# Chunk 0 of a gated attention written without moves, fewer filler products at the head, and joined products in later chunks

## The chip, the cores and the metric

The kernel runs on one core of one Trainium2 chip. The metric is device time in microseconds (us) of one execution; lower is better. Three timed executions of the kernel before gave 989.09, 989.59 and 989.59 us, median 989.59. Engines: PE is TensorE, DVE is VectorE, ACT is ScalarE, POOL is GpSimd, and SP issues the DMAs.

## What is computed

A gated linear attention (4 batches, 8 heads, 768 steps, 48 features a head) and then two feed-forward networks on its 3072 x 384 output:

```python
for t in range(S):
    state = alpha[:, :, t, :, None] * state + np.einsum('bhd,bhe->bhde', k[:, :, t], v[:, :, t])
    y[:, :, t] = np.einsum('bhd,bhde->bhe', q[:, :, t], state)
x = y.transpose(0, 2, 1, 3).reshape(B * S, H * D)
h = x @ w_in                                        # 384 -> 2048
x = np.where(h > 0, h, np.exp(np.minimum(h, 0)) - 1) @ w_out
g = x @ w_gate; val = x @ w_val                     # 384 -> 1536
return (g * sigmoid(g) * val) @ w_out2
```

All of it is float32. Large products are made of three float32r products, of high and low parts of both operands (`mm3`).

## The kernel before

The sequence is cut into 6 chunks of 128 steps, and a chunk of one batch is a **unit**: unit `u` is batch `u % 4` of chunk `u // 4`, 24 in all. Chunk 0 has no state yet, so units 0 to 3 do less than later ones. For each unit the kernel does, in the names used below:

- **load**: one DMA of 1 MB from `qkva` into a tile `in` of three buffers, with the decay F, the keys K, the queries Q and the values V. Unit 0's comes in two pieces, F (256 KB) and K, Q, V (768 KB). The tile is free for unit `u + 3` once all its readers are done.
- **decay** (methods `A`, `N`, `M`): DVE scans F (`scan`, 4 instructions), clamps it (`R<-in`), ACT makes a reciprocal, DVE and ACT refine it, and K and Q are scaled in place. From unit 4 on POOL does two of these products.
- **T**, transposes of K (`Dk`, 4 matmuls into PSUM, ACT copies them to `KT`); **S**, scores (`E`, 8 matmuls, DVE masks them into `A`); **O**, outer products of K and V (`Gs`, 8 matmuls, DVE adds them to the state `sc`); **V**, the values (`Hy`, first 4 matmuls with the state, not in chunk 0, then 8 with `A`). V's output is split into a high part (ACT) and a low part, both into the chunk's operand tile `x`. The low part is DVE's for units 4 to 23; for units 0 to 3 (`u < MINUS`) PE subtracts the high part with a product by minus the identity, and ACT copies what is left.

Of the 4 pairs of heads three lie in `x` as they come; the fourth goes to a side tile `x3`, and after each chunk `gaps` moves it with 6 DMAs into rows 48 to 63 and 112 to 127 of `x`. These rows are operands of every **h block** (`mm1`, 9 matmuls of 512 columns, then ACT and DVE make the activation `g`), and each h block is followed, two later, by an **acc block** (`mm2`, 9 matmuls that read `g`). Weights are prepared tile by tile: a DMA into one of two `raw` buffers, two passes of ACT, two of DVE (`merge`, `sign`), one of ACT and one of DVE (`wt<-raw,wt`); tile 2i is read by h blocks 2i and 2i + 1 of a chunk, tile 2i + 1 by their acc blocks. Chunks 0 and 1 go through the 2048 features in halves (`SEGMENTS`): 8 h and 8 acc blocks of chunk 0, the same of chunk 1, then the second halves. Then comes the second network, whose blocks are `gv` and `q`.

The order on each engine is not written by hand. `Plan.add` takes an operation's engine, an estimate of its time, what it reads and writes; `Plan.run` lists all of them by their longest way to the end and hands them out in that order, and `Pinned` keeps it. SP's DMAs are in one order too. While PE is planned to be idle before the first h block, `warm` puts **filler** in: products of a zero tile `wz` into `idle`, one for each 0.22 us of the planned gap. 30 more stand at the head (`at.warm(6.8)`), ahead of everything.

PSUM tags matter here: `aps` (one bank) takes T, O and V; `ape` (two banks) takes S; units 0 to 3 also use `acc0` to `acc2`.

In the trace nearly all instructions carry line L128 (the `Pinned` helper), so they are told apart by tiles: `aps<-ident,in` is T, `ape<-in` S, `aps<-in,KT` O, `aps<-in,sbd` and `aps<-A,in` V, `x<-x` the moves.

Of the kernel before, what the change touches and what calls it, by code (L numbers as in the profile page):

```python
# [8 lines left out]
F32 = mybir.dt.float32  # L9
F32R = mybir.dt.float32r  # L10
BF16 = mybir.dt.bfloat16
# [23 lines left out]
SEGMENTS += [(c, 0, NF1, (c + 1) % NCH) for c in range(2, NCH)]  # L35
MINUS = B
SOON, MARGIN = 40.0, 0.5
# [4 lines left out]
class Plan:  # L42
# [25 lines left out]
    def run(self, fill=None, until=0):  # L68
# [38 lines left out]
        for i in sorted(range(n), key=lambda i: (start[i], i)):  # L107
            if ops[i][0] == "PE" and fill and start[i] <= start[until]:
                fill(start[i] - last)
                last = start[i] + ops[i][1]  # L110
            ops[i][2]()
# [29 lines left out]
def kernel(  # L141
# [119 lines left out]
    class Attention:  # L261
        def __init__(self, es):
# [12 lines left out]
            self.bias = cp.tile([128, 2], F32, name="bias")  # L275
            self.neg = cp.tile([128, 128], F32R, name="neg")
            self.x3 = cp.tile([128, 2, TB], F32R, name="x3")
            self.u = {}
# [18 lines left out]

        def init(self):
            vec.memset(self.zero, 0.0)
# [13 lines left out]
            nc.gpsimd.tensor_copy(self.mask, t)  # L313
            for t in self.sbd:
                nc.gpsimd.memset(t, 0.0)

        def warm(self, us):

            if self.idle is None:
                self.z = self.cp.tile([128, 128], BF16, name="wz")  # L320
                vec.memset(self.z, 0.0)
# [96 lines left out]
        def Dk(self, u):  # L418
# [15 lines left out]

            plan.add("PE", 0.45, flip, r=[K], w=[key], soon=SOON, lag=MARGIN)
            plan.add("ACT", 0.48, keep, r=[key], w=["KT"])

        def E(self, u):
# [33 lines left out]

            plan.add("PE", 1.25, scores, r=[K, Q], w=keys, soon=SOON, lag=MARGIN)
            plan.add("DVE", 1.24 if len(keys) > 1 else 1.1, causal, r=keys, w=["A"])

        def Gs(self, u):
# [3 lines left out]
            c, b = divmod(u, B)  # L480
            key, bank = self.bank(u)
            sc = self.sc[b]

# [12 lines left out]
            def state():  # L496
# [6 lines left out]
                vec.tensor_tensor(out=sc[0:PR], in0=kv, in1=pc, op=ALU.mult)  # L503

            plan.add("PE", 0.75, outer, r=["KT", V], w=[key], soon=SOON, lag=MARGIN)
            plan.add("DVE", 0.65 if c else 0.3, state, r=[key, F], w=[("sc", b)])

        def Hy(self, u):
            d, (F, K, Q, V) = self.u[u], self.keys(u)
            c, b = divmod(u, B)  # L510
# [37 lines left out]
            def low():  # L548
# [7 lines left out]
            if u >= MINUS:  # L556
                plan.add("DVE", 0.74, low, r=[key], w=[xk, gk])
                return

            def minus():  # L560
                y, x3, x = parts()
                for i, h in ((slice(0, KD), x[0]), (slice(KD, NP), x3[0])):
                    ten.matmul(
                        out=d["oy"][0:PR, i.start * C:i.stop * C], lhsT=self.neg[0:PR, 0:PR],
                        rhs=h, start=False, stop=True, skip_group_check=True)

            def rest():
                y, x3, x = parts()
                act.activation(out=x3[1], in_=y[:, KD], func=AF.Copy)
                act.activation(out=x[1], in_=y[:, 0:KD], func=AF.Copy)  # L570

            plan.add("PE", 0.45, minus, r=[xk, gk], w=[key], soon=SOON)
            plan.add("ACT", 0.68, rest, r=[key], w=[xk, gk])

# [28 lines left out]
        def step(self, u):  # L603
# [5 lines left out]
            if nxt:  # L609
                self.N(u + 1)  # L610
            self.Gs(u)
# [8 lines left out]
            if nxt:  # L620
                self.Dk(u + 1)
# [3 lines left out]
    def new_x(c):  # L625
        xt[c] = P.xp.tile([128, 2, KD, TB], F32R, tag="x", name="x")
# [193 lines left out]
    w1, w2 = {}, {}  # L820
    at.warm(6.8)
    at.init()
# [241 lines left out]
```

## Time and profile before

| what | us |
|---|---|
| median of three timed runs | 989.59 |
| the profiled execution | 990.69 |
| its span (first to last instruction) | 988.9 |
| PE busy | 973.4 |
| DVE busy | 541.0 |
| ACT busy | 512.7 |
| POOL busy | 69.3 |

The sums below are made against the profiled execution, 990.69 us, of which 1.8 us lie outside the span. It is 1.1 us above the median; a difference found in it is taken from the median as it is. A busy PE is not PE at its peak, and filler counts as busy.

### The profile page before, as it was taken

What the parts mean: (1) busy time and instruction counts of PE and PEld (TensorE: products, weight loads), DVE (VectorE), ACT (ScalarE), POOL (GpSimd) and SP (SyncE); (2) the same over time, 40 slices, a digit from 0 to 9 for tenths busy, and PEclk for the clock granted to TensorE, in tenths of its full rate; (3) what the DMA queues carried; (4) which work ended last, traced back from release to release, by engine and by line L of the source; (5) the groups of instructions that cost most, each with busy time, mean ns of one, the idle gap of its engine ahead of it and who ended that gap; (6) DMA issues with size and microseconds to landing.
All of it is one profiled execution on the core that took longest, in us unless ns stands there. A gap on an engine that the chain in (4) does not pass through costs nothing.

```text
span 988.9 us, 13352 instructions
## 1 busy us (share of the span) xinstructions
PE 973.4 (98%) x5354; PEld 811.2 (82%) x5354; DVE 541.0 (55%) x840; ACT 512.7 (52%) x910; POOL 69.3 (7%) x51
## 2 busy tenths in 40 slices
PE   9899999999999999999999999999999999999997
PEld 4577788878887888888888888888888888888886
DVE  4999888667646653533677763334333334333332
ACT  3889999666776765555898542212212212212111
POOL 0122011123211310100000000000000000000000
PEclk9999999999999999999999999999999999999999
DMA  4646434333302301100434311001001001000001
GB/s 192 222 158 209 162 114 159 108 102 118 101 1 85 129 6 43 36 14 1 160 128 183 127 52 65 1 1 64 1 1 57 8 1 45 9 1 32 1 1 36
DMA packets 20662, 72.51 MB, mean 73 GB/s; under 512 B 2672, under 2 KB 5744, under 8 KB 17648
## 3 DMA queue, kind: packets, MB, share of 16 engines
q1 hardware_dynamic: 20592, 71.58, 21.2%
q8 instruction: 44, 0.72, 0.3%
q14 instruction: 26, 0.21, 0.1%
HBM read 58.20 MB, written 11.01 MB: 70 GB/s over the span
## 4 chain that ended last, share of the span: by engine, by line
PE 91%; ACT 3%; DVE 3%; DMA 2%; issue 0%; SPq 0%; ACTq 0%; DVEq 0%
PE gv L128 30%; PE acc L128 19%; PE h L128 18%; PE q L128 15%; PE aps L128 4%; PE idle L128 2%; PE ape L128 2%; DMA in<-qkva 1%; DVE in L128 1%; ACT raw L128 1%; DVE raw L128 1%; DMA raw<-w 1%; ACT e L128 1%; ACT R L128 1%; ACT x L128 0%
## 5 line engine op out<-in xcount | busy, mean ns | idle before, releaser
L128 PE MATMUL gv<-x,wt 128*128 128x512 f32 x1296 | 308.1, 391 | 0.0
L128 PEld LDWEIGHTS gv<-x,wt 128*128 128x128 f32 x1296 | 242.2, 188 | 48.0
L128 PE MATMUL h<-x,wt 128*128 128x512 f32 x864 | 215.6, 394 | 1.4 <-DMA x<-x 1.4
L128 DVE TENSOR_TENSOR s<-gv,s 128x512 f32<-128x512 f32 x144 | 99.6, 691 | 210.7 <-ACT s L128 167.3
L128 PE MATMUL acc<-g,wt 128*128 128x512 f32 x864 | 214.5, 393 | 0.2 <-DVE g L128 0.2
L128 PEld LDWEIGHTS h<-x,wt 128*128 128x128 f32 x864 | 159.7, 188 | 37.0 <-ACT r L128 1.7
L128 PEld LDWEIGHTS acc<-g,wt 128*128 128x128 f32 x864 | 160.4, 188 | 35.0 <-DVE g L128 0.6
L128 PE MATMUL q<-wt,u 128*128 128x384 f32 x864 | 163.0, 337 | 0.0
L128 PEld LDWEIGHTS q<-wt,u 128*128 128x128 f32 x864 | 153.6, 188 | 5.6
L128 ACT ACTIVATE s<-gv 128x512 f32<-128x512 f32 x72 | 43.1, 598 | 176.6 <-PE gv L128 176.6
L128 DVE SCALAR_TENSOR_TENSOR e<-e,r 128x512 f32<-128x512 f32 x96 | 68.6, 715 | 98.0 <-ACT r L128 97.9
L128 ACT ACTIVATE u<-s 128x512 fp32r<-128x512 f32 x72 | 45.4, 631 | 123.6 <-DVE s L128 123.2
L128 ACT ACTIVATE e<-h 128x512 f32<-128x512 f32 x96 | 57.1, 595 | 67.8 <-PE h L128 67.4
L128 DVE TENSOR_TENSOR g<-e,g 128x512 fp32r<-128x512 f32 x96 | 67.3, 701 | 29.8 <-ACT g L128 29.5
L128 ACT ACTIVATE g<-e 128x512 fp32r<-128x512 f32 x96 | 60.3, 628 | 28.9 <-DVE e L128 28.5
L128 DVE SCALAR_TENSOR_TENSOR raw<-raw 128x768 int32<-128x768 int32 x68 | 67.9, 1000 | 12.0 <-ACT raw L128 10.9
L128 DVE TENSOR_TENSOR u<-s,u 128x512 fp32r<-128x512 f32 x72 | 49.8, 692 | 40.6 <-ACT u L128 40.5
L128 ACT ACTIVATE e<-e 128x512 f32<-128x512 f32 x96 | 60.7, 632 | 2.9
L128 ACT ACTIVATE raw<-raw 128x768 f32<-128x768 f32 x68 | 58.9, 905 | 3.1 <-DMA raw<-w 2.9
L128 ACT ACTIVATE r<-h 128x512 f32<-128x512 f32 x96 | 55.9, 582 | 0.0
L128 POOL TENSOR_TENSOR in<-in 112x512 f32<-112x512 f32 x20 | 30.1, 1504 | 249.9 <-DVE in L128 130.7
L128 POOL TENSOR_TENSOR in<-in,R 112x512 f32<-112x512 f32 x20 | 37.0, 1849 | 79.5 <-ACT R L128 79.5
(78 smaller groups left out, 614.7 us busy)
## 6 DMA issues: line engine op xcount, KB each, us to landing
raw<-w SPq DMA_DIRECT2D x34, 768.0 KB, 4.2
in<-qkva SPq DMA_DIRECT2D x23, 1024.0 KB, 5.4
x2r<-x2d SPq DMA_DIRECT2D x18, 256.0 KB, 3.4
out<-y SPq DMA_DIRECT2D x24, 192.0 KB, 2.0
x2d<-o SPq DMA_DIRECT2D x12, 256.0 KB, 2.3
x<-x SPq DMA_DIRECT2D x36, 64.0 KB, 4.3
half<-o SPq DMA_DIRECT2D x6, 256.0 KB, 4.0
part<-half SPq DMA_DIRECT2D x6, 256.0 KB, 6.1
```

The source lines that it names most:

```text
L128: ins = getattr(self.engine, name)(*a, **k)
```

## The change

**Chunk 0 without moves.** A new method `first` takes the place of `Hy` for units 0 to 3. POOL copies parts of V (`apart`, 128 x 96) into a zeroed tile `vz`, and 4 more matmuls a unit add the fourth pair of heads straight into the rows where the moves put them. So one ACT copy, one subtraction on PE and one ACT copy are left where there were two of each, and `gaps` is not called for chunk 0. (That V's first 8 matmuls become 6, of 64 rows, and 6 more read `vz`, 12 in all.)

**Joined operations.** For units 4 to 19 T is part of the operation S, right behind it, and O part of V, right behind it, and O's output goes to `ape` instead of `aps`.

**Filler.** The 30 at the head are gone; `warm` now gets the start of the gap, and puts one for each 0.25 us into the first gap and one for each 0.36 us into later ones.

```diff
-MINUS = B
 ...
-                fill(start[i] - last)
+                fill(start[i] - last, last)
 ...
+            self.vz = cp.tile([128, 2, KD, 64], F32, name="vz")
 ...
+            nc.gpsimd.memset(self.vz, 0.0)
 ...
-        def warm(self, us):
+        def warm(self, us, start):
...
-            for _ in range(int((us - 0.2) / 0.22)):
+            for _ in range(int((us - 0.2) / (0.25 if start else 0.36))):
 ...
             # Dk
-            plan.add("PE", 0.45, flip, r=[K], w=[key], soon=SOON, lag=MARGIN)
-            plan.add("ACT", 0.48, keep, r=[key], w=["KT"])
+            if u < B:
+                plan.add("PE", 0.45, flip, r=[K], w=[key], soon=SOON, lag=MARGIN)
+                plan.add("ACT", 0.48, keep, r=[key], w=["KT"])
+            return key, flip, keep
...
             # E
-            plan.add("PE", 1.25, scores, r=[K, Q], w=keys, soon=SOON, lag=MARGIN)
+                def both():
+                    scores()
+                    flip()
+                plan.add("PE", 1.65, both, r=[K, Q], w=[*keys, key], soon=SOON, lag=MARGIN)
+                plan.add("ACT", 0.48, keep, r=[key], w=["KT"])
...
             # Gs
+            if c:
+                key, bank = ("ape",), lambda: self.pe.tile(
+                    [128, 2, 512], F32, tag="ape", name="ape")[:, 0]
...
+        def first(self, u):
...
+            def apart():
+                pool.tensor_copy(
+                    self.vz[:, :, :, D:64],
+                    d["v"][:, 2 * KD:H, 0:D].rearrange("p j (i e) -> p j i e", i=KD))
...
+                for p in range(KD):
+                    for j in range(2):
+                        ten.matmul(
+                            out=o[64 * j:64 * j + 64, p * C:(p + 1) * C], lhsT=self.vz[:, j, p],
+                            rhs=d["A"][:, j, KD], start=False, stop=p == KD - 1)
...
+            plan.add("POOL", 0.4, apart, r=[V], w=["vz"], port=True)
+            plan.add("PE", 1.5, values, r=["A", V, "vz"], w=[key], soon=SOON, lag=MARGIN)
+            plan.add("ACT", 0.45, high, r=[key], w=[xk])
+            plan.add("PE", 0.25, minus, r=[xk], w=[key], soon=SOON)
+            plan.add("ACT", 0.45, rest, r=[key], w=[xk])
...
         def Hy(self, u):
+            if u < B:
+                self.first(u)
+                return
...
-            plan.add("PE", 2.0 if c else 1.4, values, r=["A", V, Q, ("sbd", u % 2)], w=[key],
-                     soon=SOON, lag=MARGIN)
+            renew = self.Gs(u)
+            if renew:
+                okey, outer, state = renew
+                def both():
+                    values()
+                    outer()
+                plan.add("PE", 2.35, both, r=["A", V, Q, "KT", ("sbd", u % 2)], w=[key, okey],
+                         soon=SOON, lag=MARGIN)
+                plan.add("DVE", 0.65, state, r=[okey, F], w=[("sc", b)])
...
-            if b == B - 1:
+            if b == B - 1 and c:
                 self.gaps(c)
...
-    at.warm(6.8)
     at.init()
```

The plan makes a new order of this. On DVE, from the first scan to the mask of unit 0's scores (`A<-acc`); `scan` prints as `in<-in,zero`. Before:

```order
L128 SCALAR_TENSOR_TENSOR in<-in,zero 112x128 x4
L128 TENSOR_SCALAR R<-in 112x512
L128 TENSOR_TENSOR in<-in 112x512
L128 SCALAR_TENSOR_TENSOR N<-in,R 112x512
L128 TENSOR_TENSOR in<-in,R 112x512
L128 SCALAR_TENSOR_TENSOR in<-N,in 112x512
L128 SCALAR_TENSOR_TENSOR in<-in,zero 112x128 x4
L128 TENSOR_SCALAR R<-in 112x512
L128 TENSOR_TENSOR in<-in 112x512
L128 TENSOR_TENSOR A<-acc_245,mask 128x512
```

and now:

```order
L127 SCALAR_TENSOR_TENSOR in<-in,zero 112x128 x4
L127 TENSOR_SCALAR R<-in 112x512
L127 SCALAR_TENSOR_TENSOR in<-in,zero 112x128 x4
L127 SCALAR_TENSOR_TENSOR N<-in,R 112x512
L127 TENSOR_TENSOR in<-in 112x512
L127 TENSOR_TENSOR in<-in,R 112x512
L127 SCALAR_TENSOR_TENSOR in<-N,in 112x512
L127 TENSOR_TENSOR in<-in 112x512
L127 TENSOR_SCALAR R<-in 112x512
L127 SCALAR_TENSOR_TENSOR in<-in,zero 112x128 x4
L127 TENSOR_TENSOR in<-in 112x512
L127 TENSOR_TENSOR A<-acc_217,mask 128x512
```

Unit 1's scan moves ahead of unit 0's scaling, and unit 2's scan and one more scaling now stand before the mask.

On SP, the first loads of the program (x512 is unit 0's F, x1536 under `in` its K, Q and V, x2048 a whole unit, `raw` a weight tile). Before:

```order
L128 DMA in<-qkva 128x512
L128 DMA in<-qkva 128x1536
L128 DMA in<-qkva 128x2048 x2
L128 DMA raw<-w 128x1536 x2
L128 DMA in<-qkva 128x2048 x2
```

and now:

```order
L127 DMA in<-qkva 128x512
L127 DMA in<-qkva 128x2048
L127 DMA in<-qkva 128x1536
L127 DMA in<-qkva 128x2048
L127 DMA raw<-w 128x1536 x2
```

Unit 1's megabyte has gone ahead of unit 0's K, Q and V.

On PE, unit 9 (one of the units 4 to 19) between h and acc blocks; eight matmuls of O alternate in the two shapes shown. Before:

```order
L128 MATMUL aps<-ident,in 128x112 x4
L128 MATMUL h<-x,wt 128x512 x9
L128 MATMUL aps<-in,KT 64x48
...
L128 MATMUL acc_1556<-g,wt 128x512 x3
...
L128 MATMUL aps<-in,sbd_116 112x128 x4
L128 MATMUL aps<-A,in 64x128
...
L128 MATMUL h<-x,wt 128x512 x9
```

and now:

```order
L127 MATMUL ape<-in 128x128 x8
L127 MATMUL aps<-ident,in 128x112 x4
L127 MATMUL acc_1472<-g,wt 128x512 x3
...
L127 MATMUL aps<-in,sbd_116 112x128 x4
L127 MATMUL aps<-A,in 64x128
...
L127 MATMUL ape<-in,KT 64x48
...
L127 MATMUL h<-x,wt 128x512 x9
```

T, O and V were three interruptions of the blocks, and S a fourth elsewhere; now there are two.

## Rows read from the trace of the kernel before

**Rows 1.** The page: granted clock by slice, and the chain by engine.

```profile
PEclk9999999999999999999999999999999999999999
...
PE 91%; ACT 3%; DVE 3%; DMA 2%; issue 0%; SPq 0%; ACTq 0%; DVEq 0%
```

**Rows 2.** Timeline, PE: start, length, engine, line, tiles, shapes, count [idle before, releaser].

```profile
1.07 18.50 PE L128 MATMUL idle<-wz 128*128 128x512 bf16 x72 [1.07 <-DVE zero L128]
...
54.01 4.37 PE L128 MATMUL h<-x,wt 128*128 128x512 f32 x18
```

**Rows 3.** Timeline, DVE, from the first scan to the mask of unit 0.

```profile
4.77 1.37 DVE L128 TENSOR_TENSOR_SCAN in<-in,zero 112x128 f32<-112x128 f32 x4 [2.02 <-DMA in<-qkva]
...
7.77 0.69 DVE L128 TENSOR_TENSOR in<-in 112x512 f32<-112x512 f32 x1 [1.17 <-DMA in<-qkva]
8.38 0.69 DVE L128 SCALAR_TENSOR_TENSOR N<-in,R 112x512 f32<-112x512 f32 x1
...
20.76 1.29 DVE L128 TENSOR_TENSOR A<-acc,mask 128x512 int32<-128x512 int32 x2 [7.80 <-PE acc L128]
```

**Rows 4.** Busy time by stretch: length, then PE, PEld, DVE, ACT, POOL; clock, DMA share, GB/s.

```profile
9.00:10.00 1.00, 1.00 (x6) 0.48 (x5) 0.81 (x3) 0.87 (x2) 0.00 (x0) 1.00 0.97 410
...
60.00:80.00 20.00, 19.75 (x157) 15.67 (x154) 19.82 (x33) 19.81 (x38) 4.43 (x3) 1.00 0.49 184
80.00:100.00 20.00, 18.98 (x139) 15.26 (x137) 19.93 (x31) 18.58 (x35) 5.21 (x3) 1.00 0.64 199
100.00:150.00 50.00, 49.67 (x269) 40.82 (x270) 42.62 (x59) 46.52 (x80) 4.64 (x3) 1.00 0.40 136
```

**Rows 5.** Timeline, DVE: the second and the seventh low part of `g`.

```profile
71.32 0.66 DVE L128 TENSOR_TENSOR g<-e,g 128x512 fp32r<-128x512 f32 x1
...
100.94 0.68 DVE L128 TENSOR_TENSOR g<-e,g 128x512 fp32r<-128x512 f32 x1
```

**Rows 6.** Timeline, PE: second acc block; ninth h block, seventh and eighth acc blocks.

```profile
71.92 2.34 PE L128 MATMUL acc<-g,wt 128*128 128x512 f32 x9
...
100.33 2.35 PE L128 MATMUL h<-x,wt 128*128 128x512 f32 x9 [1.35 <-DMA x<-x]
102.52 2.20 PE L128 MATMUL acc<-g,wt 128*128 128x512 f32 x9
104.56 2.20 PE L128 MATMUL h<-x,wt 128*128 128x512 f32 x9
```

**Rows 7.** Timeline, PE, around unit 8's O, V and unit 9's S.

```profile
132.83 2.20 PE L128 MATMUL acc<-g,wt 128*128 128x512 f32 x9
134.96 0.67 PE L128 MATMUL aps<-in,KT 128*64 128x48 f32 x16
135.56 2.33 PE L128 MATMUL h<-x,wt 128*128 128x512 f32 x9
137.73 1.04 PE L128 MATMUL aps<-in,sbd 112*112 112x128 f32 x8
139.71 1.16 PE L128 MATMUL ape<-in 48*128 48x128 f32 x16
```

**Rows 8.** Timeline, PE's weight loads under the filler at the head.

```profile
1.90 0.15 PEld L128 LDWEIGHTS <-wz 128*128 128x128 bf16 x1 [0.28 <-issue]
...
6.59 12.48 PEld L128 LDWEIGHTS <-wz 128*128 128x128 bf16 x58 [0.28 <-issue]
```

**Rows 9.** POOL and DVE at 45 us, and POOL's copy of 128 x 128 at the head.

```profile
2.73 0.29 POOL L313 CAST mask<-mt 128x128 int32<-128x128 f32 x1
...
45.17 1.31 POOL L128 TENSOR_TENSOR in<-in,R 112x512 f32<-112x512 f32 x1 [2.10 <-ACT R L128]
...
45.27 1.76 DVE L128 SCALAR_TENSOR_TENSOR N<-in,R 112x512 f32<-112x512 f32 x1
```

**Rows 10.** Timeline, DVE and PE at the change from chunk 2 to chunk 3.

```profile
218.03 1.37 DVE L128 TENSOR_TENSOR_SCAN in<-in,zero 112x128 f32<-112x128 f32 x4 [4.23 <-DMA in<-qkva]
...
220.30 1.13 PE L128 MATMUL aps<-in,sbd 112*112 112x128 f32 x8 [0.88 <-DVE T L128]
```

More of the change, by code (lines that the diff above doesn't have):

```diff
@@ L298, in init @@
         def init(self):
+            self.z = self.cp.tile([128, 128], BF16, name="wz")
+            vec.memset(self.z, 0.0)
             vec.memset(self.zero, 0.0)
@@ L315, in init @@
                 nc.gpsimd.memset(t, 0.0)
-        def warm(self, us):
+        def warm(self, us, start):
             if self.idle is None:
-                self.z = self.cp.tile([128, 128], BF16, name="wz")
-                vec.memset(self.z, 0.0)
                 self.idle = ph.tile([128, TB], F32, tag="h", name="idle")
-            for _ in range(int((us - 0.2) / 0.22)):
+            for _ in range(int((us - 0.2) / (0.25 if start else 0.36))):
                 ten.matmul(
@@ L471, in causal @@
                     )
-            plan.add("PE", 1.25, scores, r=[K, Q], w=keys, soon=SOON, lag=MARGIN)
+            turned = self.Dk(u) if u >= B else None
+            if turned:
+                key, flip, keep = turned
+                def both():
[3 more added lines that the diff above has]
+                plan.add("ACT", 0.48, keep, r=[key], w=["KT"])
+            else:
+                plan.add("PE", 1.25, scores, r=[K, Q], w=keys, soon=SOON, lag=MARGIN)
             plan.add("DVE", 1.24 if len(keys) > 1 else 1.1, causal, r=keys, w=["A"])
@@ L503, in state, with values, high, minus @@
                 vec.tensor_tensor(out=sc[0:PR], in0=kv, in1=pc, op=ALU.mult)
+            if c:
+                return key, outer, state
             plan.add("PE", 0.75, outer, r=["KT", V], w=[key], soon=SOON, lag=MARGIN)
-            plan.add("DVE", 0.65 if c else 0.3, state, r=[key, F], w=[("sc", b)])
+            plan.add("DVE", 0.3, state, r=[key, F], w=[("sc", b)])
+        def first(self, u):
+            d, (F, K, Q, V) = self.u[u], self.keys(u)
+            key, bank = self.bank(u)
+            ts = slice(u * C, (u + 1) * C)
+            xk = ("x", 0, u)
+            def apart():
+                pool.tensor_copy(
+                    self.vz[:, :, :, D:64],
+                    d["v"][:, 2 * KD:H, 0:D].rearrange("p j (i e) -> p j i e", i=KD))
+            def values():
+                d["oy"] = o = bank()
+                for p in range(KD):
+                    for j in range(2):
+                        ten.matmul(
+                            out=o[64 * j:64 * j + 64, p * C:(p + 1) * C], lhsT=d["v"][:, 2 * p + j, :],
+                            rhs=d["A"][:, j, p], start=p == 0, stop=False)
+                for p in range(KD):
+                    for j in range(2):
+                        ten.matmul(
+                            out=o[64 * j:64 * j + 64, p * C:(p + 1) * C], lhsT=self.vz[:, j, p],
+                            rhs=d["A"][:, j, KD], start=False, stop=p == KD - 1)
+            def high():
+                if 0 not in xt:
+                    new_x(0)
+                act.activation(
+                    out=xt[0][:, 0, :, ts], in_=d["oy"][:, 0:KD * C].rearrange("p (a c) -> p a c", a=KD),
+                    func=AF.Copy)
+            def minus():
+                ten.matmul(
+                    out=d["oy"][:, 0:KD * C], lhsT=self.neg, rhs=xt[0][:, 0, :, ts],
+                    start=False, stop=True, skip_group_check=True)
+            def rest():
+                act.activation(
+                    out=xt[0][:, 1, :, ts], in_=d["oy"][:, 0:KD * C].rearrange("p (a c) -> p a c", a=KD),
+                    func=AF.Copy)
+            plan.add("POOL", 0.4, apart, r=[V], w=["vz"], port=True)
[3 more added lines that the diff above has]
+            plan.add("ACT", 0.45, rest, r=[key], w=[xk])
@@ L551, in low @@
                 vec.tensor_tensor(out=x[1], in0=y[:, 0:KD], in1=f32(x[0]), op=ALU.subtract)
-            plan.add("PE", 2.0 if c else 1.4, values, r=["A", V, Q, ("sbd", u % 2)], w=[key],
-                     soon=SOON, lag=MARGIN)
-            plan.add("ACT", 0.68, high, r=[key], w=[xk, gk])
[L556 to L573, printed above, removed]
+            renew = self.Gs(u)
[7 more added lines that the diff above has]
+                plan.add("DVE", 0.65, state, r=[okey, F], w=[("sc", b)])
+            else:
+                plan.add("PE", 2.0, values, r=["A", V, Q, ("sbd", u % 2)], w=[key],
+                         soon=SOON, lag=MARGIN)
+            plan.add("ACT", 0.68, high, r=[key], w=[xk, gk])
+            plan.add("DVE", 0.74, low, r=[key], w=[xk, gk])
         def check(self):
@@ L610, in step @@
                 self.N(u + 1)
-            self.Gs(u)
+            if u < B:
+                self.Gs(u)
             if nxt:
@@ L619, in step @@
                 self.load(u + INS)
-            if nxt:
+            if nxt and u + 1 < B:
                 self.Dk(u + 1)
```

## The prediction

> **What bounds the kernel now.** I read the chain of waits first: 91% of it is PE at a granted clock of 0.9 or more in every slice [rows 1]. So the end is PE's, and a change is worth what it takes from PE's stream or starts it earlier. The timeline of PE shows where the stream is not work: 72 filler products run from 1.07 to 19.57, and the first h block starts only at 54.01 [rows 2]. What feeds PE meanwhile is read on DVE. It does its first scan at 4.77 and is through with what it has at about 13, and then the mask of unit 0 finds it idle for 7.80 us, waiting for scores that stand in PE's queue behind the filler [rows 3]. So the filler costs, because it is longer than the time that it should fill. The table by stretch then tells who holds the pace afterwards: from 60 to 100 us DVE is busy for 39.75 of 40 us and ACT for 38.4, while from 100 to 150 DVE is busy for 42.6 of 50 [rows 4]. DVE, with ACT beside it, paces everything up to about 100 us; behind that PE alone does. Two rows show the hand-over: the seventh `g` is ready at 101.62 [rows 5], and the acc block that reads it starts at 102.52, 0.9 us later [rows 6], with no further wait for DVE behind it but one [rows 10].
>
> So a gain at the head is worth what it moves DVE, not what it moves PE, and I follow it to the seventh acc block at 102.52.
>
> **The head: DVE's lead.** The new head has 29 filler products in place of 72. In the trace the first are 0.43 us apart until 6.59, and then 58 weight loads take 12.48 us, 0.215 each [rows 8]. So 29 are over near 10.1 (13 slow ones to 6.6, 16 fast ones in 3.4), before there is anything to multiply, and the loads decide.
>
> The order of loads is new, and it is not in unit 0's favour. In the trace F and the 768 KB behind it, 1.05 MB, are on the chip when the scaling starts at 7.77 [rows 3], and transfers flow at 410 GB/s [rows 4]. If they land in the order of issue, F and unit 1 (1.31 MB) are there at 8.4, unit 0's K, Q, V (2.10 MB) at 10.3, unit 2 (3.15 MB) at 12.9. DVE's new order then runs: scan of unit 1 8.4 to 9.8; N, two scalings and the refinement at 0.61 each (the distance of two rows in [rows 3]) to 12.2, with K finished; scaling and clamp of unit 1 to 13.2; scan of unit 2 to 14.6; one scaling; mask at 15.2. PE does T and S from 12.2, in 1.7 us (S 1.16 [rows 7], T's four matmuls no more than the 0.6 of O's eight), so the scores are there at 14.0 and the mask doesn't wait. In the trace it starts at 20.76. That is 5.5 us earlier, with one scan (1.37) and one scaling (0.6) more done: **DVE leads by 7.5 us**.
>
> From there to the seventh `g` the two orders hold the same DVE operations but for these, counted row by row: up to the second `g` one more pair of `x` subtractions (0.76), up to the seventh two fewer weight passes (1.9). DVE is dense in the trace there, so its lead stays: the second `g`, 71.98 before [rows 5], comes at 71.98 - 7.5 + 0.76 = 65.2; the seventh, 101.62, at 101.62 - 7.5 - 1.9 = 92.2. ACT doesn't object: it has eight copies fewer to do by then (the fourth pair of chunk 0).
>
> PE's own way between these two: ten blocks stand between the second and the seventh acc block, at 2.04 (102.52 to 104.56, [rows 6]); two joint V and O at 2.7 (V 1.98, O 0.60, and 0.13 on the next block, [rows 7]) and one S and T at 1.7. That is 27.5, and 65.2 + 27.5 = 92.7, later than DVE's 92.2. So the seventh acc block starts at 92.7 and not at 102.52: **-9.8 us**.
>
> This holds also the end of two waits. The six moves of chunk 0 no longer stand between V of unit 3 and the first h block; by DVE's order that block starts near 42 instead of 54.01, 12 us earlier, but acc blocks can't follow faster than `g` comes, so the surplus is spent in waits of PE. It is hidden by DVE's pace; were DVE not the bound, it would be worth 2.5 more. And the ninth h block's wait of 1.35 us for chunk 1's moves [rows 6] goes, since V of unit 7 now stands five blocks ahead of it and not three: 10.2 us of cover for what took 7.8 (V's end at 92.5 to 100.33).
>
> **The joined products: -1.8 us.** Each piece of attention between blocks costs more than itself. The acc block ahead of O takes 2.13 (132.83 to 134.96) and the h block behind it 2.17, against 2.04: 0.22 for one interruption [rows 7]. Counted in the orders from the ninth h block on, there are 42 interruptions before and 31 now. Eleven at 0.13 to 0.22 are 1.4 to 2.4; priced one by one (a V has no edge ahead of it) they give 1.8. All of this stretch is PE's, so it counts in full. O's place in `ape` adds a wait of S for the state's read of it; between them stand one or more blocks, 2.04 us or more, in all units but one (5 to 6, within DVE's stretch).
>
> **What is added: +0.5 us.** POOL's copies of V are 96 columns, and the nearest row is a copy of 128 at 0.29 [rows 9]. While POOL worked for 1.31 us at 45.17, a DVE operation of 0.69 took 1.76 [rows 9], so such a copy can hold DVE for its own length: nothing at least, 4 x 0.29 = 1.2 at most; I take 0.5. The `vz` zeroing is before the first load lands. V of chunk 0 has 12 matmuls instead of 8, a third of 1.98 or 0.7 us a unit more, where PE has filler to spare: nothing, and 4 x 0.7 if that cover were gone.
>
> **Sum.** -9.8 - 1.8 + 0.5 = -11.1: the profiled 990.69 becomes 979.6. The median stands 1.1 below it, so **978.5 us**.
>
> **The rivals.**
> *More: PE keeps its lead.* If DVE's new order leaves it less to wait for than the old one did, PE is bound by its own work from the first h block at 42: 15 blocks (30.6) and four each of 1.7 and 2.7 of attention (17.6) to the seventh acc block, 90.2, so -12.3. With joins -1.8 and the 0.88 at 220 [rows 10] gone: -15, **974.5**. For it speaks that PE's surplus is 2.5 us; against it DVE's 39.75 of 40 [rows 4]. Chance 0.15.
> *Less: loads come late.* Either the new order of loads shares the bandwidth, so that unit 1 lands only with unit 0's K, Q, V at 10.3 (its scan then starts 1.9 later), or buffers of `in` come free later, because O now follows V: a wait like that of the scan at 218.03, 4.23 us on DVE and 0.88 on PE [rows 10], at each change of chunk. 2 to 3 us of the gain go: **981**. Chance 0.22.
> *Not what it says: slower, by the clock.* The filler is there to hold PE's clock up. In the trace the granted clock reads 1.00 even where filler is 0.43 apart; that distance, twice the 0.215 behind 6.59 [rows 8], shows the lower level, 1.2 GHz against 2.4. Now PE rests from 10.1 to 12.2 and has 32 filler products in place of 56 until the first h block. If it fell to the lower level there, units 0 to 3 (17.1 us of matmuls, four times 1.7, 0.6 and 1.98, and 6.9 of filler) would take 48 from 12.2 on, the first h block would start at 60.2 and, with 48.2 of work, the seventh acc block at 108.4, or some 2 later, until the clock is up: 7.9 later than before, less 1.8: **996**. It decides from 14 us of work at the lower level. Against it: between 20 and 54 the trace has short pieces and waits in turn without a slow one. Chance 0.04; a drop for a few us, which leaves -6 or so, 0.08.
> The Trainium skill speaks for this rival: "TensorE: Matmul & The Clock Gate", section "HAM oscillation", says that a kernel whose bursts of matmuls are broken by waits falls back to the slow clock at each of them. By that rule the time would be 996; no row here shows it.
>
> **How the numbers follow.** The forecast has 0.51, the larger gain 0.15, the late loads 0.22, a short drop of the clock 0.08, the slow clock 0.04. The range takes in the first three and the bounds of POOL's copies: 974 to 983. A measurement of this kernel tells some 0.2%, 2 us, from no change. All cases but the slow clock lie well below 987.6: faster 0.94, and of the clock's two cases half of the slow one and a little of the short one may end near the old time: same 0.03, slower 0.03.
>
> **What would show it.** In the changed profile: filler from 1.07 to about 10, the mask of unit 0 at 15 with no wait for PE; the first h block near 42; waits of PE before the second acc block near 65; the seventh acc block near 92.7; no `x<-x` before unit 7; from there blocks of 2.04 and interruptions of two kinds. A mask at 17 or later would say that loads bind the head; matmuls of T or S at twice their length, that the clock fell; a seventh acc block near 90 with PE dense before it, that DVE was no bound.

## The result, and the profile after

The changed kernel takes **978.44 us** (median; 977.45 to 979.42) against 989.59 (989.09 to 991.75): a ratio of 0.9886, 95% interval [0.9872, 0.9899]. That is 11.15 us less. 978.5 was forecast. The profiled execution took 977.83 with a span of 976.1, 0.6 below its median; the one of before stood 1.1 above. So between the two profiles lie 12.86 us, and the sum made on them, -11.1, is 1.76 short. The terms show more than the total does.

The page, the lines that answer to [rows 1]: the granted clock by slice, and the chain by engine.

```profile
PEclk9999999999999999999999999999999999999999
...
PE 91%; DVE 4%; ACT 2%; DMA 1%; issue 1%; SPq 0%; DVEq 0%
```

PE is still the chain. The timeline of PE answers to [rows 2, 6] (start, length, engine, line, tiles, shapes, count, and in brackets the idle time before it with its releaser):

```profile
1.07 9.23 PE L127 MATMUL idle<-wz 128*128 128x512 bf16 x29 [1.07 <-DVE zero L127]
11.52 0.57 PE L127 MATMUL aps<-ident,in 112*128 112x112 f32 x4 [1.21 <-issue]
12.07 1.16 PE L127 MATMUL acc<-in 48*128 48x128 f32 x16
...
40.48 0.44 PE L127 MATMUL acc<-x,neg 128*128 128x384 f32 x1 [1.78 <-ACT x L127]
40.77 1.36 PE L127 MATMUL idle<-wz 128*128 128x512 bf16 x3
41.57 3.70 PE L127 MATMUL h<-x,wt 128*128 128x512 f32 x9
...
65.88 0.47 PE L127 MATMUL acc<-g,wt 128*128 128x512 f32 x1
66.98 2.13 PE L127 MATMUL acc<-g,wt 128*128 128x512 f32 x8 [0.62 <-DVE g L127]
...
90.06 2.20 PE L127 MATMUL acc<-g,wt 128*128 128x512 f32 x9
92.10 2.20 PE L127 MATMUL h<-x,wt 128*128 128x512 f32 x9
94.14 2.20 PE L127 MATMUL acc<-g,wt 128*128 128x512 f32 x9
...
100.26 2.20 PE L127 MATMUL h<-x,wt 128*128 128x512 f32 x9
103.32 2.66 PE L127 MATMUL acc<-g,wt 128*128 128x512 f32 x9 [0.86 <-ACT o L127]
```

The filler ends at 10.3, and T and S of unit 0 follow at 11.52 and 12.07. The first h block starts at 41.57 instead of 54.01, but takes 3.70 us. The ninth (92.10) waits for nothing, and the seventh acc block starts at 94.14 instead of 102.52. At 103.32 there is a wait that [rows 6] do not have. On DVE, against [rows 3, 5]:

```profile
5.02 1.37 DVE L127 TENSOR_TENSOR_SCAN in<-in,zero 112x128 f32<-112x128 f32 x4 [2.15 <-DMA in<-qkva]
...
7.40 1.37 DVE L127 TENSOR_TENSOR_SCAN in<-in,zero 112x128 f32<-112x128 f32 x4 [0.55 <-DMA in<-qkva]
...
14.28 1.28 DVE L127 TENSOR_TENSOR A<-acc,mask 128x512 int32<-128x512 int32 x2
...
46.41 1.22 DVE L127 TENSOR_TENSOR A<-ape,mask 128x1024 int32<-128x1024 int32 x1 [1.40 <-PE ape L127]
...
66.25 0.68 DVE L127 TENSOR_TENSOR g<-e,g 128x512 fp32r<-128x512 f32 x1
```

The mask of unit 0 comes 6.5 us sooner and no longer waits for PE; the scores of unit 4 (46.41) keep DVE waiting instead. By stretch (length, then PE, PEld, DVE, ACT, POOL; granted clock, DMA share, GB/s), against [rows 4]:

```profile
42.00:44.00 2.00, 2.00 (x6) 1.58 (x5) 2.00 (x3) 0.89 (x2) 1.00 (x1) 0.50 1.05 392
...
60.00:80.00 20.00, 17.95 (x166) 15.02 (x165) 18.76 (x31) 16.66 (x33) 4.15 (x2) 1.00 0.52 184
80.00:100.00 20.00, 20.00 (x116) 16.71 (x115) 18.93 (x33) 16.75 (x31) 5.28 (x4) 1.00 0.62 191
```

From 80 on PE has no gap, where it had one of 1 us in twenty; so the hand-over from DVE to PE comes some 20 us sooner. From 42 to 44 the granted clock is 0.50, the level of 1.2 GHz. Behind the hand-over, the pieces of one unit's V and O, against [rows 7]:

```profile
123.82 1.04 PE L127 MATMUL aps<-in,sbd 112*112 112x128 f32 x8
124.78 1.09 PE L127 MATMUL aps<-A,in 128*64 128x128 f32 x16
125.70 0.62 PE L127 MATMUL ape<-in,KT 128*48 128x48 f32 x16
126.25 2.33 PE L127 MATMUL h<-x,wt 128*128 128x512 f32 x9
128.42 2.20 PE L127 MATMUL acc<-g,wt 128*128 128x512 f32 x9
```

V and O together take 2.43 (123.82 to 126.25), with 0.13 on the block behind: 2.56. In [rows 7] V takes 1.98, O 0.60, and the blocks around O 0.09 and 0.13 more: 2.80.

### The profile page after: what moved, and what is told of

Its sections match the earlier page's. It is cut to its first block, busy times and chain, and to the rows that moved or that the text cites. A ratio compares the mean times of both kernels' runs of the same rounds, so it can differ in the third digit from the quotient of the medians.

```text
span 976.1 us, 13264 instructions
## 1 busy us (share of the span) xinstructions
PE 957.5 (98%) x5315; PEld 808.0 (83%) x5315; DVE 543.0 (56%) x840; ACT 510.3 (52%) x902; POOL 70.1 (7%) x56
## 4 chain that ended last, share of the span: by engine, by line
PE 91%; DVE 4%; ACT 2%; DMA 1%; issue 1%; SPq 0%; DVEq 0%
PE gv L127 30%; PE acc L127 19%; PE h L127 19%; PE q L127 16%; PE aps L127 4%; PE ape L127 3%; DMA in<-qkva 1%; DVE in L127 1%; DVE raw L127 1%; ACT raw L127 0%; DVE A L127 0%; ACT e L127 0%; DVE g L127 0%; DVE e L127 0%; DVE N L127 0%
## 5 line engine op out<-in xcount | busy, mean ns | idle before, releaser
L127 DVE SCALAR_TENSOR_TENSOR raw<-raw 128x768 int32<-128x768 int32 x68 | 65.7, 969 | 11.7 <-ACT raw L127 10.5
L127 POOL TENSOR_TENSOR in<-in,R 112x512 f32<-112x512 f32 x20 | 33.8, 1691 | 81.1 <-ACT R L127 81.1
```

The costliest lines, as they stand in the source:

```text
L127: ins = getattr(self.engine, name)(*a, **k)
```

## The experiments

The change has three parts that can be made apart: the **filler** (head and spacing), the **moves** of chunk 0 (none, by the padded operand set: V of units 0 to 3 with `vz`), and the **joins** (S with T, V with O). I first built three of the other combinations and the change without its joins, then the two left over, then kernels that test what these showed. Two milestones of PE are read from each timeline: the start of the seventh acc block ("acc 7"), and the way from there to the first `gv` block, where the second network begins. The quoted expectations use other names: their chunk one is chunk 0 here and their chunk two chunk 1, VectorE is DVE and TensorE PE, a second-product block is an acc block, and the last stage is the second network.

| kernel | filler | moves gone | joins | median us (range) | sixth acc | ninth h | acc 7 | acc 7 to gv |
|---|---|---|---|---|---|---|---|---|
| before | | | | 989.59 (989.09 to 991.75) | 96.78 | 100.33 | 102.52 | 431.03 |
| e1_filler | x | | | 981.43 (980.66 to 983.66) | 88.42 | 93.27 | 96.99 | 429.69 |
| e2_moves | | x | | 991.45 (989.0 to 992.41) | 96.22 | 101.50 | 105.22 | 429.63 |
| e8_joins | | | x | 988.51 (986.55 to 990.94) | 96.62 | 101.44 | 103.56 | 427.89 |
| e4_nojoin | x | x | | 983.53 (981.99 to 986.56) | 88.07 | 94.51 | 98.23 | 429.89 |
| e6_moves_back | x | | x | 981.37 (978.56 to 983.12) | 90.21 | 95.32 | 98.88 | 426.62 |
| e3_oldfill | | x | x | 984.02 (983.05 to 985.56) | 96.73 | 98.77 | 100.81 | 426.47 |
| the change | x | x | x | 978.44 (977.45 to 979.42) | 90.06 | 92.10 | 94.14 | 426.96 |

Their ratios to the kernel before, measured beside them: e1 0.9912 [0.9895, 0.9929], e2 1.0015 [1.0004, 1.0026], e3 0.9941 [0.9923, 0.9958], e4 0.9935 [0.9915, 0.9955], e6 0.9918 [0.9903, 0.9932], e8 0.9997 [0.9987, 1.0008].

**e1_filler.** The kernel before with the new filler.

```diff
-                fill(start[i] - last)
+                fill(start[i] - last, last)
...
-            for _ in range(int((us - 0.2) / 0.22)):
+            for _ in range(int((us - 0.2) / (0.25 if start else 0.36))):
...
-    at.warm(6.8)
...
```

(`start` is 0 in the first gap, so 0.36 us is the spacing there, at the head, and 0.25 us that of later gaps; the section on the change has the two the wrong way round.)

> The kernel before with the change's filler alone (no 30 fillers at the head, 0.36 us apart up to the first score, 0.25 us afterwards); moves and separate products as before. Theory (the head's gain is VectorE's lead, brought forward by the shorter filler; the moves cost nothing once VectorE sets the pace): the mask of unit 0 starts near 14.3 us without a wait, as in the changed kernel, the seventh second-product block starts within 1 us of the changed kernel's 94.14, and the median is 980.5 to 982.5 (989.6 less 8.4, give or take 1). Rival (the moves of chunk one and their 1.35 us wait carry a good part of the gain): the seventh block stays above 98 us and the median is 985 or more.

The median is as the theory had it, 8.1 below before, and the sixth acc block starts 8.36 earlier: DVE's lead arrives in full. But acc 7, at 96.99, is a miss by both theories' reading. The timeline of PE says why:

```profile
88.42 2.20 PE L128 MATMUL acc<-g,wt 128*128 128x512 f32 x9
93.27 3.88 PE L128 MATMUL h<-x,wt 128*128 128x512 f32 x9 [2.65 <-DMA x<-x]
```

The ninth h block, the first of chunk 1, now waits 2.65 for that chunk's moves instead of 1.35 [rows 6], and then runs 3.88 us instead of 2.35. The table by stretch shows the clock in it:

```profile
94.00:95.00 1.00, 1.00 (x4) 0.71 (x3) 1.00 (x2) 0.00 (x0) 0.00 (x0) 0.50 0.92 381
```

**e2_moves** and **e4_nojoin.** The padded operand set on the kernel before, and the change with T and O as steps of their own.

```diff
...
+            if u < B:
+                self.first(u)
+                return
...
-            if b == B - 1:
+            if b == B - 1 and c:
...
```

(The diff is e2's; the lines that it leaves out are mainly `vz`, the body of `first` and the second subtraction. e4's puts T and O back as in the kernel before.)

> The kernel before with the padded operand set of chunk one alone (no moves, one subtracting product per unit, as in the change); old filler, separate products. Theory: VectorE still starts its masks at 20.8 us and sets the pace, so the seventh second-product block starts within 1 us of 102.52 and the median is 988.5 to 990.5. Rival (the moves carry a good part): the block starts at 99 us or sooner and the median is below 986.5.

> The changed kernel with transposes and outer products as separate steps again (own places in the plan and own banks, as before); new filler and no moves stay. Theory (the joins give 4 us, as the stretch from the seventh second-product block to the first of the last stage shows): 981.5 to 983.5. Rival (they give the 1.8 us of interruptions that the prediction priced): 979.5 to 981. Rival two (they only move work that stays beside other work): within 0.7 of 978.4.

Taking the moves away alone makes the kernel slower, by 1.9 us (e2 against before) or 2.1 (e4 against e1); neither theory had that. e4's 983.53 is at the upper edge of what was expected, and acc 7 shows that it came about in another way than by the joins' stretch behind acc 7. Up to the sixth acc block both gain a little (0.56 and 0.35); then the ninth h block loses it, in e2:

```profile
101.50 3.88 PE L127 MATMUL h<-x,wt 128*128 128x512 f32 x9 [3.08 <-ACT R L127]
```

and in e4:

```profile
94.51 3.88 PE L127 MATMUL h<-x,wt 128*128 128x512 f32 x9 [4.24 <-DMA x<-x]
```

(The releaser of e2's wait is the profile's guess; six moves were in flight in both.)

**e3_oldfill.** The change with the old filler.

```diff
-                fill(start[i] - last, last)
+                fill(start[i] - last)
...
-            for _ in range(int((us - 0.2) / (0.25 if start else 0.36))):
+            for _ in range(int((us - 0.2) / 0.22)):
...
+    at.warm(6.8)
...
```

> The changed kernel with the filler of the kernel before (30 at the head, then 0.22 us apart); no moves and joined products stay. Theory: the head's 8.4 us are lost again and the joins' 4 us stay, so the seventh second-product block starts near 102.5 us, and the median is 985 to 987. Rival (no moves and joins carry the gain): 979 to 981.

984.02, between the two and 1 us off the first: moves and joins together give 5.5 us, of which only 1.7 lie ahead of acc 7. There the ninth h block waits for nothing.

**e5_dense** and **e7_lump.** Does the short clock drop at the first h block cost anything?

```diff
-            for _ in range(int((us - 0.2) / (0.25 if start else 0.36))):
+            for _ in range(int((us - 0.2) / (0.18 if start else 0.36))):
```

```diff
             def minus():
+                if u == B - 1:
+                    self.warm(2.0, 1)
```

> The changed kernel with 0.18 us in place of 0.25 us per filler product behind the first score (more filler in each gap). Theory (the thin filler let the clock fall: the first h block ran 3.70 us at a granted clock of 0.50 behind a wait of 1.78 with one filler product in it, and VectorE then waited 1.40 us for the scores behind it): the first h block takes 2.2 to 2.4 us, the second second-product block starts 1 to 1.5 us sooner than 65.88, and the median is 977 to 977.5. Rival (VectorE's pace hides it, or the filler's own length delays the steps behind it): within 0.5 of 978.4, or above.

> The changed kernel with seven filler products put ahead of unit 3's subtracting product, where TensorE waits 1.78 us just before the first h block; all other filler as in the change. Theory of the clock: the first h block takes 2.2 to 2.4 us instead of 3.70, and the median is 977 to 977.5. Rival (hidden by VectorE's pace): within 0.5 of 978.4.

In both the first h block runs at the higher clock: it takes 2.42 and 2.45. e5 comes to 978.15 (977.54 to 978.69; ratio 0.9887 [0.9873, 0.9902]), the rival's value; e7 to 976.89 (976.74 to 977.9; 0.988 [0.9866, 0.9894]), the theory's. The interval of e7 overlaps that of the change, so its kernel ran again beside the change on one chip:

> The changed kernel as it is, for comparison on the same chip: 977.5 to 979.5 by every theory.

> The kernel of e7 (seven filler products ahead of unit 3's subtracting product) once more, beside the changed kernel on the same chip. Theory (the short clock drop at the first h block costs the change about 1.2 us in the end): 1 to 2 us below the changed kernel of this call. Rival (e7's 976.89 was a chip's or a call's difference): within 0.5.

978.38 (976.5 to 979.18; 0.9892 [0.9872, 0.9912]) against 978.45 (976.81 to 979.2; 0.9895 [0.9875, 0.9914]): no difference here. Over both sets of each kernel, eight executions, the medians are 977.4 and 978.4 and the ranges overlap, so a gain of up to 1 us is neither shown nor excluded. The timeline of e11 shows two other places where the clock fell:

```profile
11.59 0.58 PE L127 MATMUL aps<-ident,in 112*128 112x112 f32 x4 [2.06 <-DVE in L127]
12.14 2.08 PE L127 MATMUL acc<-in 48*128 48x128 f32 x16
...
42.43 2.41 PE L127 MATMUL h<-x,wt 128*128 128x512 f32 x9
...
66.55 3.68 PE L127 MATMUL acc<-g,wt 128*128 128x512 f32 x8 [0.62 <-DVE g L127]
```

Its table by stretch:

```profile
13.00:15.00 2.00, 2.00 (x14) 1.06 (x12) 1.97 (x6) 1.97 (x5) 0.00 (x0) 0.50 0.60 252
...
68.00:70.00 2.00, 2.00 (x6) 1.57 (x5) 1.74 (x3) 2.00 (x5) 1.13 (x1) 0.50 0.90 371
```

Right behind the filler at the head, S of unit 0 takes 2.08 instead of the change's 1.16; and at the second acc block eight matmuls take 3.68 instead of 2.13, 1.55 us more, about what the first h block had cost (3.70 - 2.2). e5 shows the same two drops (S 2.08, nine matmuls in 3.91), e7 both in part (S 1.50, eight matmuls in 3.10). Why the same waits ahead of the second acc block (0.9, 0.5 and 0.6 us in e11) end in a drop in these and in none in the change stays open.

The drop at the head stands ahead of all the filler that e5 and e7 add, so that filler didn't cause it, and it may not be what kept the first h block fast either. Ten profiled executions have the new filler at the head: the change, e10, e1, e4, e5, e6, e7, e9, e11 and e12. In seven of them (e1, e4, e5, e7, e9, e11, e12) PE idled 1.76 to 2.42 us behind it, the clock fell there, and the first h block then ran fast, in e1, e4, e9 and e12 with no filler added ahead of it. In the other three PE idled 1.02 to 1.21, the clock held at the head and fell at the first h block (in e6 in the first two). The idle time differs because the filler itself takes more or less time: the same 29 products took 9.23 us in the change and 8.08 in e5. With the old filler (before, e2, e3, e8) the clock fell at neither place. So the shorter filler buys the gain of the head with one drop early on, whose place differs from execution to execution; what e5 and e7 add is not separated from it.

**e6_moves_back** and **e8_joins.** The two combinations left: the change with chunk 0's moves, and the joins alone. Their diffs are pieces of the change's own (e6 leaves `first` and `vz` out and keeps `gaps(0)`; e8 leaves out the filler as well).

> The changed kernel with chunk one's moves and its two subtracting products back (filler and joined products stay). Theory (without joined products, the ninth h block waits for chunk two's moves, 1.35 us before, 2.65 to 4.24 with a shorter head, and it is this wait that took back part of the head's gain; joined products put five blocks behind the last value product and end it, so that chunk one's moves decide nothing): first h block at 45 to 46, no wait of the ninth, seventh second-product block at 94 to 95, median 978 to 979.5. Rival one (taking the moves away costs 2 us as it does without joined products): 976 to 977. Rival two (it gains 2.5): 980.5 to 981.

> The kernel before with the joined products alone (old filler, moves as before). Theory (joins take away the wait of the ninth h block, only 1.35 us here, put two more blocks behind the attention of chunk two, and save 3 us behind the seventh second-product block): the seventh block at 101.5 to 103, the ninth h block without a wait, median 985.5 to 987. Rival (joins give the same 5 to 7.4 us everywhere, as between the kernels without moves): 982 to 984.5.

Both miss on the slow side, e6 by 1.9 us and e8 by 1.5, and have one reason in common (e8 has another wait, of 1.62 for `g`, at 109.65). Their ninth h blocks wait, though five blocks stand between V of unit 7 and them, as in the change. In e6:

```profile
95.32 3.72 PE L128 MATMUL h<-x,wt 128*128 128x512 f32 x9 [2.91 <-DMA x<-x]
```

and in e8, without a loss of speed behind it:

```profile
101.44 2.29 PE L128 MATMUL h<-x,wt 128*128 128x512 f32 x9 [2.62 <-DMA x<-x]
```

So five blocks behind V don't end the wait by themselves. SP issues the six moves at 83.8 in e6 and at 84.0 in the change, the same time; but they land differently. The DMA issues from 80 to 90 us (operation, count, size each, median us from issue to landing), in the change:

```profile
raw<-w SPq DMA_DIRECT2D x2, 768.0 KB, 5.4
in<-qkva SPq DMA_DIRECT2D x1, 1024.0 KB, 5.4
x<-x SPq DMA_DIRECT2D x6, 64.0 KB, 4.1
```

and in e6:

```profile
raw<-w SPq DMA_DIRECT2D x2, 768.0 KB, 8.4
in<-qkva SPq DMA_DIRECT2D x1, 1024.0 KB, 10.6
x<-x SPq DMA_DIRECT2D x6, 64.0 KB, 9.7
```

The transfers are the same, but the second weight load is issued about 1.3 us later in e6, 1 us ahead of the moves instead of 2.5. From then on all of them are slow together, at 164 GB/s between 90 and 94, where loads without moves among them flow at 395 in the same stretch of e9 and at 410 in [rows 4].

**e9_behind.** The test: e6 with that weight load behind the moves.

```diff
-        plan.add("SP", 0.5, load, w=[hk, lk], kb=768)
+        plan.add("SP", 0.5, load, r=after, w=[hk, lk], kb=768)
...
-        w1[g, s] = weight(plan, lambda: P.wp, "w", w1d[g, s], 2 * NG1)
+        w1[g, s] = weight(plan, lambda: P.wp, "w", w1d[g, s], 2 * NG1, [("x", 1, B)] if i == HALF else ())
...
```

> The kernel of e6 (filler and joined products, chunk one's moves back) with one weight load, the ninth of 768 KB, issued behind chunk two's six moves instead of ahead of them. Theory (the moves are late in e6 because they share the queues with two weight loads: there they land 9.7 us after issue and the ninth h block waits 2.91 us and then runs 3.72 us at the lower clock; in the changed kernel, where the loads are ahead by another 0.7 us, they land after 4.1 and nothing waits): the moves land within 6 us of issue, the ninth h block waits less than 0.5, and the median falls from 981.4 to 977 to 978.5. Rival (the loads don't matter; the moves are late for another reason, or the block waits for something else): landing at 8 us or more, median 980.5 to 982.5.

979.19 (978.82 to 980.28), ratio 0.9905 [0.9888, 0.9922]: 2.2 below e6 and a little above the range given. The intervals of the two ratios overlap; the timelines differ by more, the first `gv` block starting at 521.56 instead of 525.50. New waits came in: 0.58 for `g` at 95.06 and 0.79 for ACT's copies at 140.97. PE's timeline:

```profile
91.75 2.20 PE L128 MATMUL h<-x,wt 128*128 128x512 f32 x9
93.98 0.49 PE L128 MATMUL acc<-g,wt 128*128 128x512 f32 x1
95.06 2.14 PE L128 MATMUL acc<-g,wt 128*128 128x512 f32 x8 [0.58 <-DVE g L128]
```

and its DMA issues from 80 to 90 us:

```profile
raw<-w SPq DMA_DIRECT2D x2, 768.0 KB, 5.4
in<-qkva SPq DMA_DIRECT2D x1, 1024.0 KB, 5.4
x<-x SPq DMA_DIRECT2D x6, 64.0 KB, 2.4
```

The moves land after 2.4, the ninth h block doesn't wait, and acc 7 starts at 93.98, where the change has 94.14; but it waits for `g` behind its first matmul, and the next h block stands at 97.03, in the change at 96.18. This kernel still has chunk 0's moves. So with the loads out of the way, taking those moves away is worth at most 0.9 us on this path, near the nothing that the prediction had; of the 4.4 us between e6 and the change at the first `gv` block (525.50 and 521.10), 3.9 came from where that one load stood.

**e12_nojoin_behind.** The same question for the joins: e4, with the load of unit 10 behind the moves.

```diff
...
-                self.load(u + INS)
+                self.load(u + INS, [("x", 1, B)] if u == 7 else ())
```

> The kernel of e4 (filler and no moves of chunk one, separate products) with the load of unit 10 issued behind chunk two's six moves instead of ahead of them. In e4 the ninth h block could start at 90.1 us, waits 4.24 for these moves and starts at 94.51, then runs 3.88 at the lower clock. Theory one (the wait is the place of the moves in the queue and the blocks left behind unit 7's value product, both): with nothing ahead of them the moves land 2.4 us after issue, as in e9, but separate products leave only three blocks behind, so the ninth block still waits 2 to 3 us: it starts at 92 to 93, the seventh second-product block at 94 to 97, median 980 to 982. Rival one (the place in the queue alone): no wait, seventh block at 92 to 92.6, median 978.5 to 979.5. Rival two (the blocks alone): as e4, 983 to 984.5.

On PE's timeline it is nearly rival one: the ninth h block starts at 90.68, after a wait of 0.3, and acc 7 at 92.85, just past its 92.6.

```profile
90.68 2.33 PE L127 MATMUL h<-x,wt 128*128 128x512 f32 x9
92.85 2.20 PE L127 MATMUL acc<-g,wt 128*128 128x512 f32 x9
```

The median, 980.04 (978.93 to 982.58), ratio 0.9913 [0.9899, 0.9928], lies in the range of theory one, though. It is 3.5 below e4, with intervals that overlap; the first `gv` block starts at 522.52 instead of 528.12. So three blocks are almost cover enough when nothing stands ahead of the moves, which land after 2.4 here too. That the blocks don't count is not shown by this. Ten kernels side by side, by the number of blocks between V of unit 7 and the ninth h block:

| kernel | blocks | moves land after (median, us) | ninth h block waits (us) |
|---|---|---|---|
| e12 | 3 | 2.4 | 0.3 |
| before | 3 | 2.4 | 1.35 |
| e1 | 3 | 4.7 | 2.65 |
| e2 | 3 | 5.5 | 3.08 |
| e4 | 3 | 6.2 | 4.24 |
| e9 | 5 | 2.4 | 0 |
| the change | 5 | 4.1 | 0 |
| e3 | 5 | 5.3 | 0 |
| e8 | 5 | 8.7 | 2.62 |
| e6 | 5 | 9.7 | 2.91 |

Both count, as theory one has it. With moves that land after 5.3 and 5.5 us, five blocks hide them (e3) and three leave a wait of 3.08 (e2). A third thing shows in the first two rows: in the kernel before, SP issues the moves 3.4 us after V ends (95.93 against 92.56), in e12 2.1 (86.14 against 84.09).

With next to no wait of the ninth h block on either side, the joined kernel is 1.3 us later at acc 7 (94.14 against 92.85) and 2.7 quicker behind it (426.96 against 522.52 - 92.85 = 429.67). That the joins cost these 1.3 is not shown: the change has the slow first h block, 1.5 us, and e12 has not.

No version here beats the change by more than its own spread. The traces point to one that might, joins behind acc 7 only with e12's order of loads ahead of it; it was not tried.

## Why the prediction was right, and where it was not

**The head: -9.8, with POOL's +0.5; measured -8.4 (102.52 to 94.14).** The reading held: DVE paced the head, the filler was longer than what it should fill, and e1 alone moves the sixth acc block by 8.36. Of the numbers inside it:

- *DVE's lead.* Given as 7.5. The mask starts at 14.28, not 15.2, because unit 1 landed a microsecond sooner (its scan at 7.40, not 8.4). By the same count the lead is 20.76 - 14.28 + 1.97 = 8.45.
- *"DVE is dense in the trace there, so its lead stays."* This is the step that failed. The second `g` is ready at 66.9, not 65.2, and with the lead of 8.45 it would have been 64.3. DVE waited 1.40 us for unit 4's scores, 0.73 at 51.37 for unit 4's outer product and 0.34 behind it: the first h block had run at the lower clock ahead of the first of these. In e7, where it ran at the higher one, the wait for the scores is gone, the other two are 0.61 and 0.33, and the second `g` is ready 1.5 us sooner, at 65.4:

```profile
64.73 0.68 DVE L127 TENSOR_TENSOR g<-e,g 128x512 fp32r<-128x512 f32 x1
```

So some 1.5 us of the lead went by the clock and 1 us by waits that the new order makes. The dense rows [rows 4] begin at 60; I had carried them back to where the new order had PE in front of DVE.
- *PE's way, 27.5 from the second acc block to the seventh.* It took 27.4, counted from 66.75 (the eight matmuls at 66.98 less one of 0.23). Right.
- *POOL's +0.5.* The four copies took 0.42 to 0.77 us each, 2.4 together, not 0.29 each; but of DVE's operations beside them three took 0.75 instead of 0.68, which makes 0.2.

**"The ninth h block's wait goes, since V of unit 7 stands five blocks ahead."** The wait went, but five blocks were only half of the reason. e3 and e2, whose moves land equally late, show that the blocks count; e6 and e8 have the five blocks and wait 2.9 and 2.6, because loads just ahead of the moves delay them further (shown for e6 by e9). The 7.8 us that I took as the time from V to the block [rows 6] is not a constant: the moves in it land after 2.4 to 9.7 us. In the change the loads happened to be far enough ahead, and that was luck. "Late loads" was a rival, but for the loads themselves, and those came sooner than forecast.

**Chunk 0's moves: "hidden by DVE's pace", worth nothing.** Nearly so: at most 0.9 us by e9 against the change. e4 was slower without the moves by the place of a load, as e12 shows. For e2 the same is likely, since its load is issued 1.9 us ahead of the moves and that of the kernel before 3.2, but no run tests it.

**The joins: -1.8, mis-sized.** Behind acc 7 the four pairs with and without joins give -2.9 (the change, e4), -3.2 (e3, e2), -3.1 (e6, e1) and -3.1 (e8, before). These hold waits that differ: 0.86, 0.41, 0.59 and 1.62 in the joined kernels, and 0.88 in the one before. Without them the four pairs give -3.8, -3.6, -3.7 and -3.9. Adding up the rows of the change and of e4 (each from its start to the next, waits apart), the blocks take about 1.8 less, which is the edges that I had priced, and the attention pieces 2.0 less, which I had put at nothing: 1.2 in V's second part, `aps<-A,in`, 0.5 in O and 0.3 in the rest. e6 and e1 give the same 1.8 and 2.0. In the rows of one unit, V takes 1.88 ahead of O (123.82 to 125.70) and took 1.98 ahead of S [rows 7], and O 0.55 for 0.60. Some of the saving is given back by a wait that I did not see coming. In the change ACT copies chunk 0's sums out late, behind work that the order puts first:

```profile
102.20 0.58 ACT L127 ACTIVATE r<-h 128x512 f32<-128x512 f32 x1
102.68 1.07 ACT L127 ACTIVATE o<-acc 128x512 f32<-128x512 f32 x2
```

The ninth acc block (103.32) waits for these copies: 1.5 us from 100.26 to 105.82, beyond two blocks of 2.04.

**The wait of [rows 10], 0.88.** Only a rival counted it. It is gone in e1, which has the filler alone, and in e2, which has the missing moves alone: acc 7 to `gv` falls by 1.3 and 1.4. Every other order here is without it, so it is no part's own gain.

**The clock.** The likeliest of the two cases was the short drop (0.08), and it happened: 3.70 us for a block of 2.2, granted clock 0.50. It came at the first h block and not at the head, where the rival had it and where seven of the ten executions with this head do show it (S of unit 0 in 2.08 us in e11). It left most of the gain, against "-6 or so", and the slow clock for good (996) did not come. The Trainium skill, "TensorE: Matmul & The Clock Gate", section "HAM oscillation", describes a kernel that falls back to the slow clock at each of its waits for the next transfer. The traces agree in part: waits of 2.65, 2.91, 3.08 and 4.24 were followed by one block at the lower level, 1.5 to 1.7 us each; a wait of 2.62 (e8) and one of 1.35 [rows 6] were not.

**The rivals.** "PE keeps its lead" (974.5) did not come: PE waited 0.97, 0.90, 0.53 and 0.62 between 55 and 67. "Slower" did not come either.

So on the profiles the head gave 0.9 less than summed (8.4 for 9.3 with POOL's share), and the way from acc 7 to `gv` 2.3 more (4.07 for 1.8: the old wait gone, a new one as long come, and PE's own work 4.05 shorter). The remaining 0.4 of the 1.76 by which the sum fell short lies behind the first `gv`. The median was met nevertheless, because the profiled execution of before stands 1.1 above its median and the one of after 0.6 below its own. The mechanism of the head was right; that the forecast is exact to 0.1 us is luck, with terms in it that are off by 1 to 2 and cancel.

## What to carry to other kernels

When a filler, a warm-up or any block at the head is shortened, follow the engine that it kept waiting, not the one that it ran on, and look for the next transfer that was late before by a little: a gain ahead of it comes through only if that transfer moves along. Before crediting a part of a change, build it alone and leave it alone out: here two parts that do nothing or harm alone give 5.5 us together (e8, e2, e3), and a single load moved behind small transfers lowered the medians of two kernels by 2.2 and 3.5. Small transfers that someone waits for go ahead of large loads that nobody waits for yet, and some blocks of other work between their source and the one that waits are still needed.

## What was not expected of the hardware

- Six moves of 64 KB landed after 2.4 us (before, e9, e12), 4.1 (the change), 6.2 (e4) or 9.7 (e6), by what else was in flight. The load ahead of them was issued 3.2 us earlier in the kernel before, some 2.5 in the change, 2.3 in e4 and 1 in e6; in e9 a single load went 2.2 us ahead, in the change and in e6 two within 3.4.
- Kernels whose ninth h block waits spread more from lowest to highest, 4.6 us in e4 and e6 and 4.4 in e8, against 2.0 and 2.4 in the change's two sets and 1.5 in e9; but e12, with a wait of only 0.3, spreads by 3.7, and e1, with one of 2.65, by 3.0. A cause is not shown.
- A wait ahead of a block doesn't alone decide the clock: 2.62 us without a drop (e8) and 2.35 ahead of one (the first two h blocks of e6, 18 matmuls in 5.95 us; in e9, behind 2.53, they take 4.34).
- With the shorter filler each of the ten profiled executions has one early drop of the clock to 0.50, at the head or at the first h block; with the old filler there is none at either place. Executions of one kernel differ by it: S of unit 0 takes 1.50 in e7 and 2.08 in e11, which have the same kernel, and acc 7 starts at 93.56 and 95.23.
